# Retention outputs of the later units as 64x64 quads, states without zero blocks, the values in two parts around a drain of TensorE

## The chip, the core and the metric

The kernel runs on one core of a Trainium2 chip. The core has TensorE (PE in the profile; its weight loads are listed apart as PEld), VectorE (DVE), ScalarE (ACT), GpSimd (POOL) and SyncE (SP, which issues most of the DMAs here). The engines run side by side, each taking its own instructions in order, and wait for each other through semaphores. The metric is the device time of one execution in microseconds (us); lower is better.

## The reference

Retention over 8 batches of 8 heads, 576 positions, head size 64, then a two-layer network with ELU over all 4608 tokens (width 512, inner width 2048). Cut to what matters:

```python
scores = scale * np.matmul(q, k.transpose(0, 1, 3, 2))
gamma = 1.0 - 2.0 ** (-5.0 - np.arange(H))
rel = pos[:, None] - pos[None, :]
Dmat = np.where(rel >= 0, gamma[:, None, None] ** rel, 0.0)
attn = np.matmul(scores * Dmat, v)                    # [B, H, S, D]
x = attn.transpose(0, 2, 1, 3).reshape(B * S, H * D)
h = x @ w_in
g = np.where(h > 0, h, np.exp(np.minimum(h, 0)) - 1)
out = g @ w_out
```

The decay splits into a factor for the query's row and one for the key's row. So a run of positions needs only the masked products inside itself and a carried state, the sum of k v^T (64x64 for each head) over all earlier positions, which the queries multiply.

## The kernel before

**Units.** The attention is cut into units: one batch `b`, 256 positions (`T` is 0 or 1, the first or second 256), four heads (`w` is 0 or 1). Eight batches give units 0 to 31 in order of `b`, `T`, `w`; the last 64 positions of each batch go into two tail items, `t0` and `t1`. Units from 12 on (`FAR`, `PAIR`) are "far" ones and go in pairs, `w` 0 and 1 together. A far unit's 256 positions are four chunks of 64, `x = 2 * e + c`: `e` is the 128-row half, `c` the partition half in it.

**What is done for a far unit.** SP loads q, k and v. POOL multiplies q and k by their decay factors into `qkn` in bf16 (`scaled`, L481) and casts v into `vn` (L531). A DMA transposes `qkn` into `qkT` (L585): eight blocks of 128 columns, four of q and four of k, in the order of `qkn`'s free axis, `(i e h d)`. A block is thus two heads (`i` in the code, 64 rows each) of one half `e`.

**Stretches.** PE works on the network most of the time and leaves it for a "stretch" (`stretch`): the outputs of the previous pair (`prevs`) and the beginnings of the next one (`its`), in this order:

- `do_inter`: the carried states times the queries. For each chunk and each pair of heads one 128x128 matmul of 64 columns: the state tile `blocks` holds the two heads' 64x64 states on its diagonal and zeros beside them. Chunk 0 of a unit with T = 0 has no earlier positions, so a pair has 12 such matmuls for T = 0 and 16 for T = 1.
- `do_scores`: 32 matmuls of 64x64 by 64 columns for the next pair, into `sc`.
- `do_values`: 32 such matmuls for the previous pair; masked scores (`pt`) by v, added to what `do_inter` left in the same PSUM tiles, `(xkey, 0)` and `(xkey, 1)`. The tile's number is the chunk's `c`, and the keys of a chunk lie in the partition half `c`, so each half of the array's rows writes one bank alone.
- `do_state`: 32 such matmuls, k by v of the next pair, into two more PSUM tiles.

There are ten stretches with a far pair in `prevs`; in the tenth `its` is the tail item `t0`, which has no states.

**After a stretch.** DVE masks the scores into `pt` (`mask_step`, L890). DVE or ACT adds up the states along the chunks (`after_far`, L834 and L836: `mid` and `end`, f32, 64 rows for each head). Then two copies of 64 partitions by 256 elements write them into the diagonal of `blocks` (`emit_z`, L849), both on the same engine, POOL, DVE or ACT. The zeros of the twelve `blocks` buffers are written once, by memsets around 24 to 40 us (L1172). ACT or DVE copies the outputs into `xt` (`put_two`, L928), which is the network's moving operand: four blocks of 128 features, each with its tokens side by side.

**The network.** `ffn1` (L273 in the profile, through the helper `mm`): 4 matmuls per step into one PSUM bank, 512 tokens wide for the later batches; then exp on ACT (`e`, L1090), max(h, 0) on ACT or DVE (L1098, L1100), and the product on DVE (`g`, L1105). `ffn2`: 16 matmuls of 512 columns for each 128 tokens, a copy to `ot` (L1139) and a store. Six PSUM banks (`"f": 6`) serve both layers, the stretch's x and state tiles, and the early transposes; the scores have the other two.

**Order.** The order on each engine is made while the kernel is built: every piece of work is an `Op` with an assumed cost for each engine that may do it, a rank, the ops that it needs, and the buffers that it takes. `Plan.run` walks through time and gives a free engine the ready op with the lowest rank; on an op with a choice of engines it takes the one that would finish first (the second number of a cost in brackets counts against that engine). `cost_of` and the cost in `stretch` are the assumed times of PE; the chip sees the order alone.

Of the kernel before, what the change touches and what calls it, by code (L numbers as in the profile page):

```python
# [17 lines left out]
P = 128  # L18
# [18 lines left out]
class Plan:  # L37
# [186 lines left out]
PE_TURN = 7  # L224
WG = ("ck11", "ck11", "ck11", "ck12")
WOG = ("ck13", "ck13", "ck13", "ck13")
FREE = ("f", "e", "g", "ot", "z")
LONE = ()

SLOTS = {  # L230
    "f": 6, "sc": 1,
    "rqk": 7, "rv": 6, "qkn": 5, "vn": 6, "qkT": 5, "pt": 3,
    "rqt": 2, "rvt": 2, "qkt": 2, "vt": 4, "qkTt": 8,
    "xt": 3, "g": 28, "e": 4, "ot": 5, "mid": 6, "end": 4, "s_mid": 6, "s_end": 10, "z": 12,
}


# [1 line left out]
def kernel(  # L239
# [234 lines left out]
    def scaled(it, i, e, cost):  # L474
        n = it.n
        key, raw = ("qkn", n), ("rq" + "qk"[i], n)
        g = ((far_q, far_k) if it.far else (gq, gk))[i]
        g = g[:, 2 * it.T + e, 4 * it.w : 4 * it.w + 4].unsqueeze(2).to_broadcast([P, 4, D])

        def emit(op):  # L480
            pin(alu[op.eng].tensor_tensor(tiles[key][:, i, e], tiles[raw][:, :, e], g, ALU.mult))  # L481
# [12 lines left out]
    def scaled_far(it, i, cost):  # L494
        n = it.n
        key, raw = ("qkn", n), ("rq" + "qk"[i], n)
        g = (far_q, far_k)[i][:, 2 * it.T : 2 * it.T + 2, 4 * it.w : 4 * it.w + 4].unsqueeze(3).to_broadcast([P, 2, 4, D])

        def emit(op):
            pin(alu[op.eng].tensor_tensor(tiles[key][:, i], tiles[raw].rearrange("p h e d -> p e h d"), g, ALU.mult))  # L500
# [54 lines left out]

    def flat(n):
        return tiles["qkn", n].rearrange("p i e h d -> p (i e h d)")

    def prepare(it, turn):
        n = it.n  # L560
# [86 lines left out]
    def do_scores(it):  # L647
        n = it.n
        sc = tiles[it.sc]
        if it.tail:  # L650
            for m in range(2):
                for hp in range(HP):
                    for i in range(2):
                        r = slice(i * D, (i + 1) * D)
                        for j in range(2):
                            tt = tiles["qkTt", n, m, j]
                            o = (m * HP + hp) * ST
                            mm(sc[j * ST : (j + 1) * ST, i, o : o + ST], tt[r, hp, ST:], tt[r, hp, :ST],
                               start=True, stop=True)
            return  # L660
        tt = tiles["qkT", n]
        if it.far:
            for x in range(4):
                for i in range(2):
                    r = slice(i * D, (i + 1) * D)
                    for c in range(2):
                        cs = slice(c * C, (c + 1) * C)
                        mm(sc[cs, i, it.sc0 + x * C : it.sc0 + (x + 1) * C], tt[r, 4 + x, cs], tt[r, x, cs], start=True, stop=True)
# [18 lines left out]
    def do_inter(it, xkey, o=0):  # L687
# [9 lines left out]
            return  # L697
        if it.far:
            tt = tiles["qkT", n]
            for x in range(4):  # L700
# [17 lines left out]
    def do_values(it, xkey, x0=0):  # L718
        n = it.n
        if it.tail:  # L720
            pt = tiles["pt", n].rearrange("p i h n -> p i (h n)")
# [10 lines left out]
        if it.far:  # L732
            pt = far_pt(it)
            for hl in range(2):
                for e in range(2):
                    for c in range(2):
                        cs = slice(c * C, (c + 1) * C)
                        o = x0 + hl * P + e * C
                        for i in range(2):
# [11 lines left out]
    def do_state(it, views):  # L751
# [3 lines left out]
        for hl in range(2):  # L755
            for e in range(2):
                for c in range(2):
# [1 line left out]
                    key, bank, ap = views[c]  # L759
                    o = (e * P if it.far else 0) + hl * D  # L760
                    for i in range(2):
                        acc(key, bank, i, ap()[i * D : (i + 1) * D, o : o + D], kn[cs, 1, e, 2 * hl + i],
                            vn[cs, 2 * hl + i, e])

    total = {}

# [53 lines left out]
    def after_far(its, st, view, bank_keys):  # L820
# [5 lines left out]
        for x in range(4):  # L826
# [15 lines left out]
            prev = run, key  # L842
            if m == 2:
                out = key_of(name, b, t, 0, *((x + 1,) if x < 3 else ()))

                def emit_z(op, key=key, out=out):
                    for j in range(2):
# [3 lines left out]
                blk = add(f"b{x}_{n}", {"POOL": 0.8, "DVE": (0.52, 1.0), "ACT": (0.76, 0.6)}, [run, zeros], emit_z, its[0].rank + 3,  # L851
                          take=[T("z", out, [P, 2, 2, P], BF16)], use=[key])
                for it in its:
                    if x < 3:
                        it.bms.append(blk)
                    else:
                        it.be = blk
# [48 lines left out]
    def inter_deps(it):  # L906
        if it.tail:
            return [*it.cvs, *(at[4 * it.t + j, 1, w].be for j in range(4) for w in range(2))]
        return [it.cv, *(it.bms if it.far else [it.bm])] + ([at[it.b, 0, it.w].be] if it.T else [])

    def inter_uses(it):
        if it.tail:
# [5 lines left out]

    xdone, xbegun = {}, set()

    def put_two(its, xkey, dep):

        for c in range(2):
            it = its[0]

            def emit(op, c=c, it=it):
                dst = tiles[it.xt][:, :, it.T * TB : (it.T + 1) * TB].rearrange("p h (e c r) -> p c h e r", e=2, c=2)[:, c]
                pin(copy[op.eng](dst, tiles[xkey, c].rearrange("p (h e r) -> p h e r", e=2, r=C)))  # L928

            first = it.xt not in xbegun  # L930
            xbegun.add(it.xt)
# [5 lines left out]
    def put_x(it, xkey, dep):  # L937

        for c in range(2):
            def emit(op, c=c):  # L940
# [3 lines left out]
                    pin(copy[op.eng](dst, xs.rearrange("p (m h n) -> p m h n", m=2, h=HP)))  # L944
                else:
                    src = xs[:, : 2 * P].rearrange("p (h e r) -> p h e r", h=2, e=2)
                    o = it.T * TB + c * P
                    dst = xt[:, 2 * it.w : 2 * it.w + 2, o : o + P].rearrange("p h (r e) -> p h e r", e=2)
                    if it.far:
                        dst = xt[:, 2 * it.w : 2 * it.w + 2, it.T * TB : (it.T + 1) * TB].rearrange(  # L950
                            "p h (e c r) -> p c h e r", e=2, c=2)[:, c]
                    pin(copy[op.eng](dst, src))  # L952

            first = it.xt not in xbegun
# [29 lines left out]
    def stretch(prevs, its):  # L984
# [86 lines left out]
    def ffn1(blk, p, rank):  # L1071
# [243 lines left out]
```

## Time and profile before

| | |
|---|---|
| time, median of three runs | 301.13 us (300.9 to 301.63) |
| the profiled execution | 301.73 us; span 300.0 us; granted clock 1.0 |
| matmuls of the network, 512 columns | start 0.216 us apart |
| a stretch, first `blocks` matmul to the end of the states' issue | about 1.3 us (T = 0) and 1.4 us (T = 1) |
| `emit_z` copies, 64x256 | POOL 64 at 0.399 us, ACT 16 at 0.404 us |
| `qkn` of far units, 128x256 | POOL 80 at 0.614 us |
| first layer's exp, ACT / max, ACT or DVE / product, DVE | 0.597 / 0.594 or 0.695 / 0.684 us |
| copies to `xt` of a pair, 128x512 | ACT 20 at 0.589 us |
| memsets of `blocks` | DVE 12 at 0.272 us |
| sums of states, 128x256 | DVE 0.415 to 0.425 us |

The page gives for each engine the time in which it was busy. A matmul's duration in it is the time from its start to a modelled end; matmuls of one stream overlap, so what one costs is read from the distance of starts. A line of the timeline is a run of equal instructions: start, length, engine, line, operation, output <- inputs, array size, shape and number; brackets at the end say how long the engine was idle before and who ended that. In the list of waits each line is: engine and line that waited <- who ended it: us in all, times, longest. A few per cent of matmul records are missing from a trace (here 536 of 576 full-width matmuls of the second layer have one), so counts can fall short and a gap of one matmul's length may be none.

### The profile page before, as it was taken

How to read it: one execution, taken by the hardware profiler on the slowest of the kernel's cores; microseconds unless marked ns; L12 is line 12 of the kernel's file. 1: busy time of each engine (PE TensorE's matmuls, PEld its weight loads, DVE VectorE, ACT ScalarE, POOL GpSimd, SP SyncE). 2: the span in 40 equal slices, each digit the busy share in tenths (PEclk: the TensorE clock that was granted, in tenths of full speed). 3: DMA queues.
4: the chain of work that ended last, by engine and by line, in shares of the span. 5: the costliest groups of instructions: out<-in, count | busy, mean ns of one | idle time of the engine just before them, and what ended most of it. 6: DMA issues, size and time to landing. Idle time of an engine off the chain costs nothing.

```text
span 300.0 us, 8468 instructions
## 1 busy us (share of the span) xinstructions
PE 291.4 (97%) x3371; PEld 169.9 (57%) x3405; DVE 174.3 (58%) x312; ACT 194.6 (65%) x379; POOL 145.0 (48%) x276
## 2 busy tenths in 40 slices
PE   8999999899999999999999999999999999999996
PEld 4778746658767764545545544554545444444444
DVE  5979945948756637697755663675442564334300
ACT  2449724827768758787676777768764676777611
POOL 5980389975757838599393974536330000000000
PEclk9999999999999999999999999999999999999999
DMA  7999999999999999999999989876762010011132
GB/s 203 264 206 211 219 294 298 260 196 206 181 169 250 220 177 240 214 214 195 224 209 210 210 188 214 149 170 78 185 147 75 14 38 35 35 35 37 35 106 70
DMA packets 135607, 50.10 MB, mean 167 GB/s; under 512 B 108176, under 2 KB 131088, under 8 KB 135568
## 3 DMA queue, kind: packets, MB, share of 16 engines
q1 hardware_dynamic: 131344, 45.37, 72.7%
q0 software_dynamic: 4224, 4.19, 8.4%
q8 instruction: 26, 0.43, 0.6%
q14 instruction: 13, 0.11, 0.1%
HBM read 36.70 MB, written 9.44 MB: 154 GB/s over the span
## 4 chain that ended last, share of the span: by engine, by line
PE 89%; POOL 3%; DMA 2%; DVE 2%; issue 1%; ACT 0%; ACTq 0%; DVEq 0%
PE f L273 86%; PE sc L273 3%; DMA qkT<-qkn 2%; POOL qkn L481 1%; DVE pt L896 1%; PE f L544 1%; POOL s_end L794 1%; POOL s_mid L794 1%; POOL w_in_sb L459 0%; DVE qkn L481 0%; POOL vn L531 0%; DVE xt L952 0%; DVE qkT L550 0%; DVE s_mid L808 0%; PE f L1276 0%
## 5 line engine op out<-in xcount | busy, mean ns | idle before, releaser
L1105 DVE SCALAR_TENSOR_TENSOR g<-e,f 128x512 bf16<-128x512 f32 x144 | 96.4, 684 | 79.6 <-ACT f L1098 79.0
L273 PE MATMUL f<-w_out_sb,g 128*128 128x512 bf16 (+2 forms) x584 | 138.7, 367 | 2.4 <-issue 1.6
L273 PE MATMUL f<-xt,w_in_sb 128*128 128x256 bf16 (+1 forms) x758 | 139.6, 325 | 0.6 <-DVE xt L952 0.2
L1090 ACT ACTIVATE e<-f 128x512 f32<-128x512 f32 x144 | 85.0, 597 | 47.8 <-PE f L273 39.5
L273 PEld LDWEIGHTS <-w_in_sb 128*128 128x128 bf16 x768 | 74.3, 98 | 53.2 <-DVE xt L952 0.5
L273 PEld LDWEIGHTS <-g 128*128 128x128 bf16 x608 | 56.8, 98 | 58.5
L1098 ACT ACTIVATE f<-f 128x512 f32<-128x512 f32 x122 | 72.2, 594 | 0.0
L1139 ACT COPY ot<-f 128x512 f32<-128x512 f32 (+2 forms) x38 | 21.4, 567 | 19.1 <-PE f L273 16.3
L849 POOL CAST blocks<-mid 64x256 bf16<-64x256 f32 x48 | 19.1, 398 | 18.4 <-DVE mid L836 9.1
L481 POOL TENSOR_TENSOR qkn<-rqk,far_q 128x256 bf16<-128x256 f32 x40 | 24.0, 614 | 7.4 <-DMA rqk<-in_q_dram 6.7
L481 POOL TENSOR_TENSOR qkn<-rqk,far_k 128x256 bf16<-128x256 f32 x40 | 24.1, 614 | 5.5 <-DMA rqk<-in_k_dram 5.0
L531 POOL CAST vn<-rv 128x512 bf16<-128x512 f32 x28 | 17.1, 612 | 15.8 <-DMA rv<-in_v_dram 15.6
L481 POOL TENSOR_TENSOR qkn<-rqk,gq 128x256 bf16<-128x256 f32 x21 | 13.0, 626 | 12.5 <-DMA rqk<-in_q_dram 11.6
L1100 DVE TENSOR_SCALAR f<-f 128x512 f32<-128x512 f32 x22 | 15.3, 695 | 4.3 <-ACT e L1090 4.0
L896 DVE TENSOR_TENSOR pt<-sc,mask 128x1024 bf16<-128x1024 f32 x12 | 14.6, 1216 | 5.3 <-PE sc L273 5.2
L928 ACT CAST xt<-f 128x512 bf16<-128x512 f32 x20 | 10.7, 589 | 9.7 <-PE f L273 9.7
L601 POOL TENSOR_TENSOR qkt<-rqt,gq 128x256 bf16<-128x256 f32 x16 | 9.4, 614 | 12.7 <-DMA rqt<-in_k_dram 12.5
L481 POOL TENSOR_TENSOR qkn<-rqk,gk 128x256 bf16<-128x256 f32 x21 | 12.8, 628 | 2.4 <-DMA rqk<-in_k_dram 2.4
L890 DVE TENSOR_TENSOR pt<-sc,mask_t 128x1024 bf16<-128x1024 f32 x10 | 12.2, 1220 | 2.2 <-PE sc L273 2.2
L952 ACT CAST xt<-f 128x256 bf16<-128x256 f32 x17 | 6.9, 450 | 9.2 <-PE f L273 9.2
L273 PE MATMUL sc<-qkT 64*64 64x64 bf16 (+1 forms) x512 | 9.7, 208 | 0.9 <-DMA qkT<-qkn 0.8
L836 DVE TENSOR_TENSOR mid<-f,mid 128x256 f32<-128x256 f32 x20 | 8.5, 425 | 3.3 <-ACT mid L834 1.0
(88 smaller groups left out, 174.3 us busy)
## 6 DMA issues: line engine op xcount, KB each, us to landing
out_dram<-ot SPq DMA_DIRECT2D x30, 256.0 KB, 3.1
rqk<-in_q_dram SPq DMA_DIRECT2D x40, 128.0 KB, 3.3
rqk<-in_k_dram SPq DMA_DIRECT2D x40, 128.0 KB, 3.3
rv<-in_v_dram SPq DMA_DIRECT2D x40, 128.0 KB, 3.5
rqk<-in_q_dram SPq DMA_DIRECT2D x12, 256.0 KB, 5.5
rqk<-in_k_dram SPq DMA_DIRECT2D x12, 256.0 KB, 5.3
rv<-in_v_dram SPq DMA_DIRECT2D x12, 256.0 KB, 10.2
w_in_sb<-in_moe_w_in_dram POOLq DMA_DIRECT2D x4, 512.0 KB, 9.2
```

The source lines that it names most:

```text
L273: pin(nc.tensor.matmul(*a, **kw))
L481: pin(alu[op.eng].tensor_tensor(tiles[key][:, i, e], tiles[raw][:, :, e], g, ALU.mult))
L531: pin(copy[op.eng](tiles["vn", n], tiles["rv", n]))
L849: pin(copy[op.eng](tiles[out][r, :, :, r], tiles[key][r]))
L890: pin(nc.vector.tensor_tensor(tiles[it.pt].rearrange("p i h n -> p (i h n)")[:, : 2 * w * C].rearrange("p (i x n) -> p i x n", i=2, n=C), ...
L896: pin(nc.vector.tensor_tensor(tiles["pt", n].rearrange("p i h n -> p (i h) n"), tiles[it.sc].rearrange("p i (h n) -> p (i h) n", h=2), mas ...
L928: pin(copy[op.eng](dst, tiles[xkey, c].rearrange("p (h e r) -> p h e r", e=2, r=C)))
L1090: pin(nc.scalar.activation(tiles[ekey], tiles[hkey], AF.Exp))
L1098: pin(nc.scalar.activation(ph, ph, AF.Relu))
L1100: pin(nc.vector.tensor_scalar_max(ph, ph, 0.0))
L1105: pin(nc.vector.scalar_tensor_tensor(tiles[gkey], tiles[ekey], -1.0, tiles[hkey], ALU.add, ALU.min))
L1139: pin(copy[op.eng](tiles[okey][:, :cols], tiles[pkey][:, :cols]))
```

## The change

Far units (12 to 31) alone change, except for the `xt` layout, which changes for all.

1. `qkn` of a far unit gets the order `(i h e d)`, so a block of `qkT` is one head, with `e` = 0 in rows 0 to 63 and `e` = 1 in rows 64 to 127. Scores and states read it accordingly.
2. The carried states are kept as plain 64x64 blocks in a new tile `y`, in the partition half `e` of the chunk that will use them. Both heads of a pair lie beside each other; there are no zeros. Each sum is written by two ops of one copy each, 64 partitions by 256 elements: the one that stays in its partitions may go to POOL, DVE or ACT, the one that crosses partitions to DVE or ACT. Only the last state of a batch (read by the tails) stays a `blocks` tile, so six buffers and six memsets are left of twelve.
3. `do_inter` of a far unit takes four 64x64 matmuls, one for each quadrant of the array (`e` in rows, head `i` in columns), where one of 128x128 stood for two heads: 24 for each T = 0 pair, 32 for each T = 1 pair. The PSUM tile's number is now `e`.
4. With that, half of the values (keys of partition half `c` into tile `e` with `c` different from `e`) would have the other rows of the array write the same bank. `do_values` is called twice: `c = e` straight after the states' products, and the rest after `nc.tensor.drain()` at the end of the stretch. The order in a stretch is now: inter, 16 values, scores, states, drain, 16 values.
5. `xt` holds its tokens by blocks of 128, `(t k n)`: a copy writes 512 contiguous elements, and the first layer's moving operand is four (or two) pieces of 128.
6. The assumed PE cost of a far unit's inter part falls to 0.1, and the order of all engines is planned anew with it.

```diff
-FREE = ("f", "e", "g", "ot", "z")
+FREE = ("f", "e", "g", "ot", "z", "y")
...
-    "xt": 3, "g": 28, "e": 4, "ot": 5, "mid": 6, "end": 4, "s_mid": 6, "s_end": 10, "z": 12,
+    "xt": 3, "g": 28, "e": 4, "ot": 5, "mid": 6, "end": 4, "s_mid": 6, "s_end": 10, "z": 6, "y": 7,
...
+    def by_head(n):
+        return flat(n).rearrange("p (i h e d) -> p i h e d", i=2, h=4, e=2)
...
-            pin(alu[op.eng].tensor_tensor(tiles[key][:, i, e], tiles[raw][:, :, e], g, ALU.mult))
+            dst = by_head(n)[:, i, :, e] if it.far else tiles[key][:, i, e]
+            pin(alu[op.eng].tensor_tensor(dst, tiles[raw][:, :, e], g, ALU.mult))
...
-            for x in range(4):
-                c, e = x % 2, x // 2
-                if it.T + x == 0:
-                    continue
-                s = kept("s_mid", it.b, it.T, it.w, x) if x else kept("s_end", it.b, 0, it.w)
-                for hl in range(2):
-                    acc((xkey, c), 0, 2, tiles[xkey, c][:, o + hl * P + e * C : o + hl * P + (e + 1) * C], s[:, hl],
-                        tt[:, e * 2 + hl, c * C : (c + 1) * C])
+            for hl in range(2):
+                for c in range(2):
+                    for i in range(2):
+                        for e in range(2):
+                            x, r = 2 * e + c, slice(e * D, (e + 1) * D)
+                            if it.T + x == 0:
+                                continue
+                            s = kept("s_mid", it.b, it.T, it.w, x) if x else kept("s_end", it.b, 0, it.w)
+                            at0 = o + hl * P + c * C
+                            acc((xkey, e), 0, i, tiles[xkey, e][i * D : (i + 1) * D, at0 : at0 + C], s[r, 2 * hl + i],
+                                tt[r, 2 * hl + i, c * C : (c + 1) * C])
...
-                for e in range(2):
+                for i in range(2):
                     for c in range(2):
-                        cs = slice(c * C, (c + 1) * C)
-                        o = x0 + hl * P + e * C
-                        for i in range(2):
-                            acc((xkey, c), 0, i, tiles[xkey, c][i * D : (i + 1) * D, o : o + C], vn[cs, 2 * hl + i, e],
-                                pt[cs, i, 2 * e + hl])
+                        cs, e = slice(c * C, (c + 1) * C), c ^ cross
+                        o = x0 + hl * P + c * C
+                        acc((xkey, e), 0, i, tiles[xkey, e][i * D : (i + 1) * D, o : o + C], vn[cs, 2 * hl + i, e],
+                            pt[cs, e, 2 * hl + i])
...
+                if x < 3 or t == 0:
+                    half = slice((x + 1) // 2 % 2 * D, ((x + 1) // 2 % 2 + 1) * D)
+                    blk = []
+                    for j in ((x + 1) // 2 % 2, 1 - (x + 1) // 2 % 2):
+                        def emit_y(op, key=key, out=out, j=j, half=half):
+                            dst = tiles[out].rearrange("p w (l j) d -> p w l j d", j=2)[half, :, :, j]
+                            pin(copy[op.eng](dst, tiles[key][j * D : (j + 1) * D]))
+
+                        cost = {"DVE": (0.3, 0.6), "ACT": (0.4, 0.4)}
+                        blk.append(add(f"b{x}{len(blk)}_{n}", cost if blk else {"POOL": 0.41, **cost}, [run], emit_y,
+                                       its[0].rank + 3, take=[] if blk else [T("y", out, [P, 2, 4, D], BF16)],
+                                       use=[key, *([out] if blk else [])], after=blk[0] if blk else None))
...
+    def by_block(key):
+        return tiles[key].rearrange("p k n -> p (k n)").rearrange("p (t k n) -> p t k n", k=KJ, n=P)
...
-                dst = tiles[it.xt][:, :, it.T * TB : (it.T + 1) * TB].rearrange("p h (e c r) -> p c h e r", e=2, c=2)[:, c]
-                pin(copy[op.eng](dst, tiles[xkey, c].rearrange("p (h e r) -> p h e r", e=2, r=C)))
+                pin(copy[op.eng](by_block(it.xt)[:, 2 * it.T + c], tiles[xkey, c].rearrange("p (h n) -> p h n", n=P)))
...
-            return ("i" in parts) * (0.27 + 0.06 * it.T) + 0.1 * sum(x in parts for x in "svt")
+            return 0.1 * sum(x in parts for x in "isvt")
...
         def emit(op):
+            far = bool(prevs) and prevs[0].far
             for i, it in enumerate(prevs):
                 do_inter(it, xkey, *([i * 2 * P] if len(prevs) > 1 else []))
+            if far:
+                for i, it in enumerate(prevs):
+                    do_values(it, xkey, i * 2 * P, 0)
             for it in its:
                 do_scores(it)
-            for i, it in enumerate(prevs):
-                do_values(it, xkey, *([i * 2 * P] if len(prevs) > 1 else []))
+            if not far:
+                for i, it in enumerate(prevs):
+                    do_values(it, xkey, *([i * 2 * P] if len(prevs) > 1 else []))
             if states:
                 for it in its:
                     do_state(it, view_of(it))
+            if far:
+                pin(nc.tensor.drain())
+                for i, it in enumerate(prevs):
+                    do_values(it, xkey, i * 2 * P, 1)
...
-                    o, x = (ph, xt[:, j]) if wide else (ph[:, f * TB : (f + 1) * TB], xt[:, j, at0 : at0 + TB])
+                    if blk == "T":
+                        o, x = ph, xt[:, j]
+                    else:
+                        x = by_block(xkey)[:, at0 // P : (2 * TB if wide else at0 + TB) // P, j]
+                        o = ph if wide else ph[:, f * TB : (f + 1) * TB]
+                        o = o.rearrange("p (t n) -> p t n", n=P)
```

In the changed order PE's instructions are the same up to the first stretch with a far pair in `prevs`. Behind it the stretches keep their sequence but stand between other MLP matmuls; after the last tail item 52 matmuls of the first layer follow each other, where there were 32.

More of the change, by code (lines that the diff above doesn't have):

```diff
@@ L662, in do_scores @@
         if it.far:
-            for x in range(4):
-                for i in range(2):
-                    r = slice(i * D, (i + 1) * D)
+            for h in range(4):
+                for e in range(2):
+                    r = slice(e * D, (e + 1) * D)
                     for c in range(2):
                         cs = slice(c * C, (c + 1) * C)
-                        mm(sc[cs, i, it.sc0 + x * C : it.sc0 + (x + 1) * C], tt[r, 4 + x, cs], tt[r, x, cs], start=True, stop=True)
+                        mm(sc[cs, e, it.sc0 + h * C : it.sc0 + (h + 1) * C], tt[r, 4 + h, cs], tt[r, h, cs],
+                           start=True, stop=True)
             return
@@ L699, in do_inter @@
             tt = tiles["qkT", n]
-            for x in range(4):
-                c, e = x % 2, x // 2
-                if it.T + x == 0:
-                    continue
-                s = kept("s_mid", it.b, it.T, it.w, x) if x else kept("s_end", it.b, 0, it.w)
-                for hl in range(2):
-                    acc((xkey, c), 0, 2, tiles[xkey, c][:, o + hl * P + e * C : o + hl * P + (e + 1) * C], s[:, hl],
-                        tt[:, e * 2 + hl, c * C : (c + 1) * C])
+            for hl in range(2):
+                for c in range(2):
+                    for i in range(2):
+                        for e in range(2):
+                            x, r = 2 * e + c, slice(e * D, (e + 1) * D)
[5 more added lines that the diff above has]
+                                tt[r, 2 * hl + i, c * C : (c + 1) * C])
             return
@@ L716, in do_inter, with do_values @@
                         queries(n, slice(0, P), hl, c))
-    def do_values(it, xkey, x0=0):
+    def do_values(it, xkey, x0=0, cross=None):
         n = it.n
@@ L761, in do_state @@
                     for i in range(2):
-                        acc(key, bank, i, ap()[i * D : (i + 1) * D, o : o + D], kn[cs, 1, e, 2 * hl + i],
-                            vn[cs, 2 * hl + i, e])
+                        k_of = by_head(n)[cs, 1, 2 * hl + i, e] if it.far else kn[cs, 1, e, 2 * hl + i]
+                        acc(key, bank, i, ap()[i * D : (i + 1) * D, o : o + D], k_of, vn[cs, 2 * hl + i, e])
     total = {}
@@ L844, in after_far @@
                 out = key_of(name, b, t, 0, *((x + 1,) if x < 3 else ()))
+                if x < 3 or t == 0:
[9 more added lines that the diff above has]
+                                       use=[key, *([out] if blk else [])], after=blk[0] if blk else None))
+                    for it in its:
+                        if x < 3:
+                            it.bms += blk
+                        else:
+                            it.be = blk
+                    continue
                 def emit_z(op, key=key, out=out):
@@ L853, in after_far @@
                 for it in its:
[L854 to L857, printed above, removed]
+                    it.be = blk
                 continue
@@ L908, in inter_deps @@
             return [*it.cvs, *(at[4 * it.t + j, 1, w].be for j in range(4) for w in range(2))]
-        return [it.cv, *(it.bms if it.far else [it.bm])] + ([at[it.b, 0, it.w].be] if it.T else [])
+        return [it.cv, *(it.bms if it.far else [it.bm])] + (
+            [] if not it.T else at[it.b, 0, it.w].be if it.far else [at[it.b, 0, it.w].be])
     def inter_uses(it):
@@ L946, in emit @@
                     src = xs[:, : 2 * P].rearrange("p (h e r) -> p h e r", h=2, e=2)
[L947 to L951, printed above, removed]
+                    hs = slice(2 * it.w, 2 * it.w + 2)
+                    dst = by_block(it.xt)[:, 2 * it.T + c, hs].rearrange("p h (r e) -> p h e r", e=2)
                     pin(copy[op.eng](dst, src))
```

7 lines of the change are left out of this document (4 added, 3 removed).

## The prediction

> **What bounds the kernel now.** I read the page first (busy shares, the slices, the chain), then who waited for whom on TensorE (PE), then the timeline of PE in two of the ten stretches that the change touches, then the rows of single operations.
>
> ```profile
> PE 291.4 (97%) x3371; PEld 169.9 (57%) x3405; DVE 174.3 (58%) x312; ACT 194.6 (65%) x379; POOL 145.0 (48%) x276
> PE   8999999899999999999999999999999999999996
> PE 89%; POOL 3%; DMA 2%; DVE 2%; issue 1%; ACT 0%; ACTq 0%; DVEq 0%
> ```
>
> PE is busy 97% of the span and 89% of the chain is PE. A busy PE alone proves little, so the waits:
>
> ```profile
> PE f L273 <- issue: 1.6, 10, 0.2
> PE f L273 <- DVE zero L278: 1.3, 1, 1.3
> PE sc L273 <- DMA qkT<-qkn: 0.8, 1, 0.8
> PE f L544 <- POOL qkn L481: 0.3, 1, 0.3
> PE f L273 <- DVE xt L952: 0.2, 1, 0.2
> ```
>
> The four named releasers lie in the first 60 us. The ten waits on "issue" of 0.16 us are no waits: each stands where PE goes back to 128x128 work, and is the place of one matmul whose record is missing (the next one starts 216 ns, one 512-column matmul, late). So from 60 to 297 us PE issues without a pause, and what the change adds to or takes from PE's own stream moves the end by the same amount. Work on DVE, ACT, POOL and SP counts only if it makes PE wait.
>
> The part at stake is the stretch, in which PE leaves the MLP for the attention of one pair of units. Outputs of a pair with T = 0, then the start of one with T = 1:
>
> ```profile
> 124.25 0.51 PE L273 MATMUL f<-qkT,blocks 128*128 128x64 bf16 x12
> 124.70 0.45 PE L273 MATMUL sc<-qkT 64*64 64x64 bf16 x32
> 124.97 0.44 PE L273 MATMUL f<-pt,vn 64*64 64x64 bf16 x32
> 125.23 0.52 PE L273 MATMUL f<-vn,qkn 64*64 64x64 bf16 x32
> 125.68 0.82 PE L273 MATMUL f<-xt,w_in_sb 128*128 128x512 bf16 x2
> ...
> 110.61 0.63 PE L273 MATMUL f<-qkT,blocks 128*128 128x64 bf16 x16
> 111.17 0.45 PE L273 MATMUL sc<-qkT 64*64 64x64 bf16 x32
> ```
>
> Durations of pipelined matmuls overlap, so I price by starts. Twelve state matmuls take 124.70 - 124.25 = 0.45 us, sixteen 111.17 - 110.61 = 0.56: four more cost 0.11, some 28 ns each (the trace's single starts say 29). 12 x 0.029 = 0.35, so 0.095 of either block is the change from 128x128 to 64x64 work. The 32 scores take 0.27 us, the 32 values 0.26: 8.3 ns per quad matmul. The 32 states take 0.34, and the way back to 128x128 some 0.12.
>
> **The quads.** Removed are the 140 matmuls of `blocks` by `qkT` (5 stretches of 12, 5 of 16); added are 280 of 64x64 (24 and 32). By the scores' row 32 quads cost 0.27. For 24, both lower quadrants still do all eight rounds, so they cost between 24/32 of 0.27 = 0.20 and 0.27; I take 0.24. The 0.095 of the mode change stays; it now comes ahead of the quads instead of behind. Saved: 0.56 - 0.095 - 0.27 = 0.195 for T = 1, 0.45 - 0.095 - 0.24 = 0.115 for T = 0. Sum 5 x 0.195 + 5 x 0.115 = 1.55 us (1.4 to 1.7).
>
> If the quads ran no closer than the matmuls of `blocks`, 29 ns apart, 280 x 29 = 8.1 us would replace 140 x 29 = 4.1, and the part would lose 4.0 us instead; the scores' row, 8.6 ns, contradicts that for quads of four different tiles. A rule of the Trainium skill speaks against the quads too (TensorE: Matmul & The Clock Gate, Part 1): it puts the start-to-start distance of matmuls at no less than about 25 ns, however few columns, by which they would take 7.0 us and lose 2.9. This trace differs from it by a factor of three.
>
> **The drain.** `nc.tensor.drain()` stands in all ten stretches, between the states (the tail's scores in the tenth) and the second half of the values. No drain between matmuls is in this trace. The nearest row is the one at the program's end (rows of its line: times min/median/max in ns, first and last start; then the last matmuls of the timeline):
>
> ```profile
> L1310 PEldq DRAIN  x2: 13/604/1195, 296.1 to 299.6; - x2
> ...
> L1299 PEldq DRAIN  x1: 8/8/8, 0.3 to 0.3; - x1
> ```
>
> ```profile
> 295.77 1.45 PE L273 MATMUL f<-w_out_sb,g 128*128 128x128 bf16 x23
> ```
>
> The long one starts at 296.07, while PE's queue still holds matmuls, and lasts 1.195 us, to 297.27: 0.05 after the last matmul's end (295.77 + 1.45 = 297.22). So a drain holds PE's sequencer until the array is through. A 64-column matmul lasts 0.193 from its start; add that 0.05, and 0.05 until the next instruction starts, as PE restarts after a memset in the chain:
>
> ```profile
> 1.21 0.05 issue
> 1.26 3.17 PE f L273 x7
> ```
>
> The second half of the values then starts 0.29 after the last state instead of 0.01: 0.28 lost, 2.8 us in ten stretches. PE runs in order, so nothing on PE hides it. Queued behind the drain are the 16 values, the whole MLP stream, and the x banks: values used to end ahead of the 32 states, now they end the stretch, so ACT's copies to `xt` start 0.34 later against the MLP stream. In the stretch at 110.61 these copies end at 113.05 and the MLP first reads that `xt` at 113.89; of 0.84 us 0.5 stays, so nothing is added. If ACT is late by more than that, PE waits there, at most two or three times by some tenths.
>
> Bounds. Below: a drain costs what the mode change costs, 0.095, so 0.95 in all; or nothing, as the drain at the start (8 ns, on an empty array). Above: with 0.1 for the sequencer's next step (on PE, 0.10 passes from the end of a semaphore instruction at 299.48 to the drain at 299.58) and 0.04 for 16 values that can no longer be loaded ahead (the states need 0.34 per 32 where the values need 0.26), it is 0.42, so 4.2. I take 0.28, the row of the same instruction, and half of the 0.04, so 0.2, for the slower second half.
>
> For the low bound there is a rule as well: the Trainium skill (TensorEngine Tiling (Array Packing), Tiling Modes) says that changing the tiling mode drains TensorE. By it the 0.095 is the price of a drain, and the sum falls by 2.0 us. What the rule doesn't say is whether an explicit drain, which goes through the sequencer, can be that short; the row at 296.07 says no.
>
> **What lies beside PE, at nothing.** The state copies are 80 before (64 on POOL, 16 on ACT) and 80 after: in the changed order 38 on POOL, 32 on ACT, 10 on DVE. At 0.40 each ACT gains 16 x 0.404 = 6.5 us and loses five relus of 0.594 to DVE; DVE gains those five at 0.695 and ten copies at about 0.415 (its nearest row, 128x256 from PSUM), and loses six memsets of 0.272. ACT goes from 195 to 198 us, DVE from 174 to 180, both far under PE's 291; POOL falls by 10. The copies follow the sums by a few us, and the stretch that reads them comes 7 to 20 us later. The new element order of `qkn` gives POOL a destination in four pieces; strided sources cost it 0.626 against 0.614 without, so 80 x 0.01 on an engine half idle. `xt` by blocks makes the MLP's moving operand four pieces of 128 columns. Scores of early units read two pieces of 64 and repeat every 56 ns per four quads, as do their values, which read 128 in one piece: no price.
>
> PE's order is the same up to the first far stretch; the third stands eight MLP matmuls (1.7 us) earlier. Its last transpose was issued at 118.60 and lands 4.3 us later, 1.8 before the scores at 124.70; with two drains ahead of it that still holds, so nothing. If that cover is gone, it costs what is missing, at most 1 us, once.
>
> **Sum.** -1.55 + 2.8 + 0.2 = +1.45 us. The profiled execution took 301.73 us (span 300.0, 1.7 around it), 0.6 over the median 301.13; it should become 303.2 with a span of 301.5, and the median 302.6.
>
> **The rivals.**
> - The drain is as short as a mode change (0.095). For it: both wait for the array to run empty. Against: the drain at 296.07. -1.55 + 0.95 = -0.6, so 300.5.
> - The other side, faster: the drain holds nobody up, because by the time the sequencer reaches it the array is through, or the matmuls behind it are taken as if it weren't there. For it: 8 ns at the start. Against: PE runs its queue well behind the sequencer (1.2 us at the end). -1.55, so 299.6. It decides once a drain costs under 0.06.
> - ACT and DVE become the bound in long runs of first-layer matmuls. The changed order has 52 in a row (13 steps of 0.864 us) after the last tail, 32 before. Per 13 steps, ACT has 13 exps and 8 relus (21 x 0.597 = 12.5 us), DVE 13 x 0.684 + 5 x 0.695 = 12.4, PE 11.2: they fall 1.3 behind. Six PSUM slots hold 5.2 us, less one in filling and some 2.2 of exp, relu, product (0.60 + 0.59 + 0.68) and hand-offs: 2.1 of slack, so they cover it. If the tail's banks take two slots, 1.7 is gone and PE waits 0.9 there and about as much in the run of 36 in the middle: 304.4.
> - The quads don't overlap, 29 ns apart. Against: the scores' row. 301.13 + 4.0 + 3.0 = 308.1.
>
> **How the numbers follow.** Forecast 0.60 (own range 301.9 to 303.6: drain 0.24 to 0.36), short drain 0.15, free drain 0.12, ACT and DVE 0.12, no overlap 0.01. The range reaches from the short drain to ACT and DVE, 300.5 to 304.4. A measurement tells 0.3%, 0.9 us, from no change. Slower: 0.55 of the forecast plus 0.13 = 0.68; same: 0.05 + 0.15 = 0.20; faster: 0.12.
>
> **What would show it.** The rows of `y` by `qkT` should take 0.27 per 32 by starts; from the last state to the values behind the drain should pass about 0.3 us, ten times; PE's waits should name no engine after 60 us. A gap of 0.1 or less makes it wrong; so do waits on ACT or DVE around 235 us, or quads that start 25 ns or more apart.

## The result, and the profile after

The changed kernel took 304.75 us (median of 4 runs, 303.98 to 305.75) against 301.28 for the kernel before beside it: ratio 1.0112, 95% interval 1.0077 to 1.0147. It is slower, as forecast, but by 3.5 us where 1.45 were forecast, and outside the range. A second measurement, among the experiments below, gave 303.96 against 301.23, ratio 1.0085 (1.0071 to 1.0098): 2.55 us by the ratio (the medians lie 2.73 apart). Both intervals hold 1.0077 to 1.0098, 2.3 to 2.9 us, and that is the loss to be explained.

From the page of the changed kernel: busy time and share by engine, TensorE's (PE's) busy tenths in 40 slices, and the engines' shares of the chain of waits.

```profile
PE 294.8 (97%) x3545; PEld 167.6 (55%) x3545; DVE 179.8 (59%) x322; ACT 196.2 (65%) x389; POOL 135.4 (45%) x250
PE   7999999999899999999999999999999999999996
PE 75%; DMA 14%; POOL 6%; DVE 3%; issue 1%; SPq 1%; ACT 0%; POOLq 0%; ACTq 0%
```

PE still bounds it; ACT, DVE and POOL are about where the prediction put them (198, 180, 135). The fall of PE's share in the chain from 89% to 75% looks like news and is not: the chain in order of time is PE, with the drains between, from 77.45 us to the last matmul, and only before that does it run mostly over transfers and POOL, where executions differ (below). What PE waited for (total us, times, longest us):

```profile
PE f L273 <- issue: 1.7, 8, 0.4
PE f L273 <- DVE zero L278: 1.3, 1, 1.3
PE f L273 <- POOL s_mid L802: 0.9, 1, 0.9
PE sc L273 <- DMA qkT<-qkn: 0.5, 1, 0.5
PE f L273 <- DVE pt L919: 0.2, 1, 0.2
PE f L273 <- DVE vn L533: 0.2, 1, 0.2
PE f L546 <- POOL qkn L482: 0.2, 1, 0.2
```

The named waits end at 77.45 us, with the one on `s_mid`. The prediction's sign, no engine after 60 us, was thus missed by this one wait; in the stretches no engine is named. "issue" now stands for the drains, as the timeline of one stretch shows (start us, us, engine, line, operation; what is in brackets is idle time behind the modelled end):

```profile
111.71 0.45 PE L273 MATMUL f<-qkT,y 64*64 64x64 bf16 x32
111.98 0.30 PE L273 MATMUL f<-pt,vn 64*64 64x64 bf16 x16
112.11 0.47 PE L273 MATMUL sc<-qkT 64*64 64x64 bf16 x32
112.39 0.45 PE L273 MATMUL f<-vn,qkn 64*64 64x64 bf16 x32
113.03 0.32 PE L273 MATMUL f<-pt,vn 64*64 64x64 bf16 x16 [0.19 <-issue]
113.28 0.39 PE L273 MATMUL f<-w_out_sb,g 128*128 128x512 bf16 x1
```

The quads are as forecast: 32 states by query in 111.98 - 111.71 = 0.27 us. Behind the 32 new states the second half of the values starts at 113.03. The states themselves end their starts at 112.66, so 0.37 us pass where 0.01 passes between two quads.

For all runs I use one account of PE's matmul starts: when the first attention stretch after 84 us begins; the time of that and the twelve further stretches up to the end of the attention (each from 0.216 us behind the start of the last MLP matmul ahead to the start of the next MLP matmul, a missing record counted as 0.216); and the rest.

| kernel | first stretch at | 13 stretches | rest | last start |
|---|---|---|---|---|
| before | 85.42 | 17.99 | 193.59 | 297.00 |
| after | 86.18 | 20.16 | 193.67 | 300.01 |

The rest, all MLP matmuls, differs by 0.08 (it is 193.56 to 193.67 in all twelve profiles of this case), so `xt` by blocks, the copies and the new order cost nothing there, as forecast. Of 3.0 us, 0.76 arose before 86 us and 2.17 in the stretches. The first are mostly the wait on `s_mid` (0.9), here in the chain in order of time (start, us, what):

```profile
71.72 4.42 DMA rqk<-in_q_dram
...
76.21 0.61 POOL qkn L482
76.82 0.58 POOL s_mid L802
...
78.08 8.49 PE f L273 x88
```

A load took 4.42 us, POOL took its `qkn` only then and the `s_mid` behind it, and PE waited. The experiments had to settle whether the first belongs to the change, and why the second is not 1.45.

### The profile page after: what moved, and what is told of

Its sections match the earlier page's. It is cut to its first block, busy times and chain, and to the rows that moved or that the text cites. A ratio compares the mean times of both kernels' runs of the same rounds, so it can differ in the third digit from the quotient of the medians.

```text
span 303.0 us, 8828 instructions
## 1 busy us (share of the span) xinstructions
PE 294.8 (97%) x3545; PEld 167.6 (55%) x3545; DVE 179.8 (59%) x322; ACT 196.2 (65%) x389; POOL 135.4 (45%) x250
## 4 chain that ended last, share of the span: by engine, by line
PE 75%; DMA 14%; POOL 6%; DVE 3%; issue 1%; SPq 1%; ACT 0%; POOLq 0%; ACTq 0%
PE f L273 73%; DMA w_out_sb<-in_moe_w_out_dram 7%; POOL qkn L482 2%; DMA qkT<-qkn 2%; PE sc L273 2%; DMA rv<-in_v_dram 2%; DMA rqk<-in_k_dram 2%; DMA rqk<-in_q_dram 1%; DVE pt L919 1%; POOL s_mid L802 1%; POOL s_end L802 1%; POOL w_out_sb L467 1%; POOL vn L533 1%; POOL w_in_sb L459 0%; DVE qkn L482 0%
## 5 line engine op out<-in xcount | busy, mean ns | idle before, releaser
L273 PE MATMUL f<-w_out_sb,g 128*128 128x512 bf16 (+2 forms) x608 | 141.7, 368 | 0.1
L1135 ACT ACTIVATE f<-f 128x512 f32<-128x512 f32 x117 | 69.2, 594 | 0.0
L1137 DVE TENSOR_SCALAR f<-f 128x512 f32<-128x512 f32 x27 | 18.7, 695 | 4.2 <-ACT e L1127 3.9
L859 POOL CAST y<-mid 64x256 bf16<-64x256 f32 x24 | 9.8, 409 | 23.9 <-DVE mid L844 11.3
L954 ACT CAST xt<-f 128x512 bf16<-128x512 f32 x18 | 9.8, 588 | 14.7 <-PE f L273 14.7
L273 PE MATMUL f<-pt,vn 64*64 64x64 bf16 (+1 forms) x512 | 11.5, 204 | 2.2 <-issue 1.7
L859 ACT CAST y<-mid 64x256 bf16<-64x256 f32 x30 | 11.7, 402 | 0.5
```

Source lines behind the costliest of these rows:

```text
L273: pin(nc.tensor.matmul(*a, **kw))
L859: pin(copy[op.eng](dst, tiles[key][j * D : (j + 1) * D]))
L954: pin(copy[op.eng](by_block(it.xt)[:, 2 * it.T + c], tiles[xkey, c].rearrange("p (h n) -> p h n", n=P)))
L1135: pin(nc.scalar.activation(ph, ph, AF.Relu))
L1137: pin(nc.vector.tensor_scalar_max(ph, ph, 0.0))
```

## The experiments

Ten runs: eight new kernels, and both kernels once more. Each was timed beside the kernel before on the same chip.

**A drain alone, in the kernel before.** In all ten stretches:

```diff
             for it in its:
                 do_scores(it)
+            if prevs and prevs[0].far:
+                pin(nc.tensor.drain())
             for i, it in enumerate(prevs):
                 do_values(it, xkey, ...)
```

> The kernel before, with a drain of TensorE in each of the ten stretches of units 12 to 31, between the scores and the values; nothing else is changed. Theory (a drain costs what the changed kernel's trace shows from the last state to the first value behind it, 0.39 us, less the 0.01 that two quads stand apart): ten times 0.38, so 3.8 us, ratio 1.0126, and a gap of 0.37 to 0.39 us from the last score to the first value in each of the ten. Rival (the drain costs the 0.28 of the prediction, and what is missing lies elsewhere): 2.8 us, ratio 1.009. The page's waits stay as before.

Measured: 303.86, ratio 1.0075 (1.0048 to 1.0102). Timeline of its stretch at 110 us, and the row of the drain's line (times min/median/max in ns, first and last start):

```profile
110.63 0.45 PE L273 MATMUL sc<-qkT 64*64 64x64 bf16 x32
111.21 0.44 PE L273 MATMUL f<-pt,vn 64*64 64x64 bf16 x32
111.47 0.49 PE L273 MATMUL f<-vn,qkn 64*64 64x64 bf16 x32
```

```profile
L1016 PEldq DRAIN  x10: 410/414/420, 95.0 to 213.0; - x10
```

From the first score to the first value 0.58 us pass instead of 0.27. The single starts give a gap of 0.326 or 0.327 in nine of ten (0.329 in the other) instead of 0.022, and the states behind take 0.30 instead of 0.34. The 13 stretches take 20.74, against 17.93 in a second profile of the kernel before: 0.28 per drain. So the theory with 0.38 fell; at this place the prediction's 0.28 is right, in part by luck: the gap grew by 0.30, and the faster states give 0.03 back. The starts also show its parts: the drain ends 0.073 us after the last score's modelled end, and the next matmul starts 0.060 after that (0.05 and 0.05 had been put in).

**The drains taken out.** VectorE copies one element of an x bank behind the first half, and the second half, which writes that bank, waits for the copy; this keeps the halves in order.

```diff
+    spare = const.tile([1, 2], FP32, name="spare")
...
                     do_values(it, xkey, i * 2 * P, 0)
+                pin(nc.vector.tensor_copy(spare[:, :1], tiles[xkey, 1][:1, :1]))
...
-                pin(nc.tensor.drain())
```

> The changed kernel without its ten drains. In the place of each drain VectorE copies one element of the x bank behind the first half of the values, and the second half waits for that copy, so the halves stay in order; between them lie the scores and states, about 0.55 us. Theory (the drain is the whole loss): the gap from the last state to the second half falls from 0.39 to 0.01 us where the copy comes in time, so 3.8 us come back, 301.0, ratio to the kernel before 0.999; if VectorE takes the copy late by 0.2 to 0.3 us in every stretch, as an operation of 0.6 us may stand ahead of it, 303 to 304. Rival (the drain is worth 2.8 and the rest is the changed order): 302.0 where the copies come in time, ratio 1.003.

Measured: 300.51, ratio 0.9976 (0.9954 to 0.9998).

```profile
110.11 0.47 PE L273 MATMUL sc<-qkT 64*64 64x64 bf16 x32
110.40 0.47 PE L273 MATMUL f<-vn,qkn 64*64 64x64 bf16 x32
110.69 0.34 PE L273 MATMUL f<-pt,vn 64*64 64x64 bf16 x16
```

```profile
L1041 DVE COPY spare<-f x10: 145/145/147, 95.1 to 214.3; 1x1 f32<-1x1 f32 x10
```

The second half follows the first state by 0.29 us instead of 0.64. The copy takes 0.145 us and is in time in nine stretches; in the tenth, where no states lie between the halves, the second half starts 0.18 behind the last score instead of 0.02. The stretches take 17.40 us, 2.85 less than in the changed kernel measured again (below). The time lies under both numbers that were expected where the copies come in time, 301.0 and 302.0: the gaps are the theory's, the 2.85 us are close to the rival's 2.8, and the rest of the difference in time lies outside the stretches. The same with ScalarE's copy:

> The changed kernel without drains, the second half of the values waiting for a copy of one element of the x bank by ScalarE (with VectorE in this place the time was 300.5, ratio 0.998). Theory (all that the drains cost comes back, whoever does the copy, if it is there within the 0.55 us of scores and states): 300.2 to 300.8 with a gap of 0.01 us in nine stretches. Rival (ScalarE takes it late, behind an exp or a relu of 0.6 us): gaps of 0.1 to 0.5 us in most stretches, 301 to 303.

Measured: 300.49, ratio 0.9976 (0.9964 to 0.9989), stretches 17.42, a gap of 0.01 in nine: theory. Both versions beat both kernels.

**Two drains in a row.** The line is there twice.

> The changed kernel with two drains in a row in place of each. Theory (a drain costs the emptying of the array, which the second finds empty, and a step of the sequencer): the second adds at most 0.1 us, so 0 to 1 us in ten, 304.8 to 305.8. Rival (each drain has a fixed price of its own): 0.38 more each, 3.8 us, 308.5.

Measured: 303.89, ratio 1.0093 (1.0061 to 1.0125). That is under the 304.8 to 305.8 expected, which had been counted from the first measurement of the changed kernel, and too wide to tell the two apart; the trace does.

```profile
L1050 PEldq DRAIN  x10: 13/13/13, 97.0 to 219.3; - x10
```

The second drain lasts 13 ns and lengthens the usual gap from 0.373 to 0.451: 0.08. So the rival's fixed price of 0.38 falls: most of a drain's price is the emptying of the array, and the rest is this step.

**The drain ahead of the scores.**

```diff
                     do_values(it, xkey, i * 2 * P, 0)
+                pin(nc.tensor.drain())
...
-                pin(nc.tensor.drain())
```

> The changed kernel with the drain right behind the first half of the values, ahead of the scores, instead of behind the states; the second half of the values follows the states at once. Theory (a drain waits for what the array still holds; behind the states it ends 0.126 us after their last modelled end, behind the scores only 0.073): a gap of 0.32 to 0.33 us at the drain, 0.01 from the states to the second half, and 0.03 to 0.05 us less per stretch, so 0.3 to 0.5 us under the changed kernel. Rival (the price of a drain doesn't hang on its place): no difference.

Measured: 302.99, ratio 1.0065 (1.005 to 1.0079), 0.97 us under the changed kernel; stretches 19.38 against 20.25. More came back than the theory gave. Gaps of 0.32 stand in three stretches and 0.305 in the last, but 0.355 in three and 0.40 to 0.44 in the other three. So at the drain the theory's 0.32 to 0.33 came in three stretches only. What came back beside it are pauses inside the rows of quads: there are none over 0.045 us in this kernel, and 0.67 of the 0.87 us come from stretches six, eight, nine and ten, where the changed kernel measured again has its pauses and longest gaps. That they matter was not in any theory so far.

**The planner's cost alone.** The kernel before with the changed cost of a stretch, and the changed kernel with the old one:

```diff
-            return ("i" in parts) * (0.27 + 0.06 * it.T) + 0.1 * sum(x in parts for x in "svt")
+            return 0.1 * sum(x in parts for x in "isvt")
```

> The kernel before, with the changed kernel's cost of a stretch in the planner (the order of instructions changes, the work doesn't). Theory (the order is worth nothing, and the early wait of 0.9 us on POOL at 76 us is a late transfer of that one execution): 301.2, ratio 0.997 to 1.003. Rival (the order planned for shorter stretches brings the early wait and the rest of the loss): about 0.8 us slower, ratio 1.0025 or more, and a wait of PE on POOL of 0.5 us or more near 76 us in its trace.

> The changed kernel with the planner's old cost of a stretch, so the order of its instructions is planned as for the kernel before; the work is the changed kernel's. Theory (order is worth nothing): the same as the changed kernel within 0.3%. Rival (the order brings 0.7 us or more of the loss): 0.7 us or more under it.

Measured: 300.89, ratio 0.9992 (0.9966 to 1.0018), no wait of PE on POOL over 0.4 us in its trace; and 304.13, ratio 1.0101 (1.0077 to 1.0125). The order by itself is worth nothing that these can tell.

**Both kernels again.**

> The changed kernel itself, once more, beside the others. Theory (its steady loss is in the ten stretches, where its trace shows 2.2 us more than the kernel before, and the 0.8 us that it lost before 86 us is a late transfer of that execution, as the first stretch begins at 84.5 and at 85.7 us in two kernels with the same instructions up to there): 303.4, ratio 1.0065 to 1.0085. Rival (the early loss belongs to the change): 304.7, ratio 1.0115, and a first stretch at 86 us or later in its trace.

> The kernel before itself, once more, as a measure of scatter. Theory (what stands ahead of 86 us scatters by 0.8 us between executions and the rest doesn't): ratio 0.999 to 1.001; a first stretch between 84.5 and 86.2 us; at most one pause of 0.06 us or more inside the ten stretches, and their sum with the three others 17.8 to 18.0 us. Rival (the stretches scatter as well): a sum off by 0.3 us or more.

Measured: 303.96, ratio 1.0085 (1.0071 to 1.0098), first stretch at 85.50, so between the two times that were expected, with the first stretch ahead of the rival's 86; and 301.19, ratio 0.9998 (0.9981 to 1.0014), first stretch at 86.08. So the unchanged kernel, too, comes as late as the changed one did in the first profile. The longest of its waits there:

```profile
PE f L273 <- ACT vn L531: 1.7, 1, 1.7
```

One `vn` that came 1.7 us late in this profile is not in the list of the first one. Over all profiles the first stretch begins between 84.2 and 86.1 us in the kernel before and its variants (five) and between 84.5 and 88.0 in the changed kernel and its variants (seven). The two versions without drains say that this is scatter: their instructions are those of the changed kernel up to the stretches, and over 25 runs they took 0.7 us less than the kernel before, of which the stretches explain some 0.55. A loss ahead of the stretches that belongs to the change would have made them slower than that, as far as an interval of 0.4 us to either side tells.

**Longer rows of quads in the kernel before.** The account of the starts shows single steps of 0.06 to 0.18 us inside rows of 64x64 matmuls, at no semaphore and not at a drain. To see whether the row's length brings them, the scores of the ten stretches are issued twice:

```diff
-            for it in its:
+            for it in its * (2 if prevs and prevs[0].far else 1):
                 do_scores(it)
```

> The kernel before, with the 32 scores of each of the ten stretches issued twice (the second time they write the same values), so that 128 matmuls of 64x64 follow each other (96 in the last) instead of 96 (64). Theory (a long row of quads outruns what feeds TensorE's queue: seven kernels with 112 to 120 quads in a row show pauses of 0.06 to 0.16 us inside them, 0.3 to 0.7 us in all, three with 96 in a row only one of 0.11): 2.7 us for the scores, and pauses of 0.06 us or more in at least three of the ten stretches, none ahead of the 57th quad, so 3.0 to 3.4 us more than the kernel before, ratio 1.010 to 1.011. Rival (the pauses come from the state copies and the changed order, not from the row's length): 2.7 us and at most one pause, ratio 1.009.

Measured: 304.23, ratio 1.0099 (1.008 to 1.0118); stretches 21.30, 3.37 more than in the kernel before again. Two stretches of the same kind from its timeline, behind their 12 state matmuls:

```profile
146.59 0.71 PE L273 MATMUL sc<-qkT 64*64 64x64 bf16 x64
147.12 0.45 PE L273 MATMUL f<-pt,vn 64*64 64x64 bf16 x32
147.39 0.52 PE L273 MATMUL f<-vn,qkn 64*64 64x64 bf16 x32
...
170.93 0.71 PE L273 MATMUL sc<-qkT 64*64 64x64 bf16 x64
171.46 0.45 PE L273 MATMUL f<-pt,vn 64*64 64x64 bf16 x32
171.73 0.67 PE L273 MATMUL f<-vn,qkn 64*64 64x64 bf16 x32
```

The same 128 quads; only the states last 0.67 instead of 0.52, for a pause of 0.142 between two of them. Such a pause stands in five of the ten stretches (0.095, 0.142, 0.114, 0.182, 0.134), none ahead of the 80th quad of its row. Scores twice cost 0.267 in a clean stretch (1.697 against 1.430), 2.7 in ten; the pauses bring the remaining 0.7. The time alone, 2.4 to 3.6 us by its interval, fits theory and rival. The trace doesn't fit the rival, at most one pause, and the order on every engine is that of the kernel before here, but for the doubled scores. (The expectation counts the earlier rows as 112 to 120 quads; they are 104 to 128, and in the kernel with the drain ahead of the scores 40 to 80, without a pause.)

The single starts tell more. Each row begins in groups of four, one quad for each quadrant of the array: steps of 3, 4, 3 and 22 ns as a rule, so a quadrant starts a quad every 32 ns. Between the 51st and the 63rd quad the groups end, in every row that neither a drain nor a wait cuts before, and even steps of 8 to 9 ns follow, with longer ones of 17 to 34 among them. All 30 pauses of 0.06 us or more that no semaphore explains, in nine profiles, stand behind the last group of their row; behind a drain the groups are back. This looks like a lead of waiting instructions that a row uses up, so that a late instruction is felt only behind it; that reading fits all rows here, but no run tested it.

## Why the prediction was right and wrong

The account for the ten stretches, per stretch, from those without a pause (kernel before again; without drains; changed kernel again): with T = 0 1.430, 1.337, 1.65; with T = 1 1.547, 1.37, 1.69.

- **The quads** were right. They save 1.430 - 1.337 = 0.09 and 1.547 - 1.37 = 0.18, the slower second half included: 5 x 0.09 + 5 x 0.18 = 1.35. The prediction's terms, -1.55 + 0.2, are -1.35. That the net fits so well is in part chance: in the drainless kernel the 32 scores start over 0.28 us instead of 0.25 and the 32 states over 0.28 instead of 0.34, and neither was forecast. That matmuls can't start closer than some 25 ns, as the Trainium skill has it (TensorE: Matmul & The Clock Gate, Part 1), does not hold for the new rows as a whole, which start 8 ns apart on average. For one quadrant it holds, at 32 ns; the prediction compared the rule with all four at once.
- **The drain** was right in its mechanism and a little small. Behind the states it costs 1.65 - 1.337 = 0.31 and 1.69 - 1.37 = 0.32, so 3.15 instead of 2.8. The gap alone, 0.37 as a rule, overstates it: with the drain the rows ahead of and behind it run 0.05 faster by their starts. Behind the scores it costs 0.28. The gaps differ by how late the drain ends after the last modelled end ahead of it, 0.126 behind states against 0.073 behind scores; why states leave the array later was not tried. Where a pause stands among the states just ahead (stretch eight of the changed kernel, in both its profiles), it is only 0.05 to 0.06, as if there were a backlog that a pause works off.
- **The short drain and the free drain**, rivals, are out. The mode change ahead of the quads is 0.094 and the drain 0.28 to 0.32. The Trainium skill's rule that a change of tiling mode drains TensorE (TensorEngine Tiling (Array Packing), Tiling Modes) is therefore no price for an explicit drain.
- **ACT and DVE as the bound**, a rival, is out: no wait of PE on them after 60 us in the list above (the two of 0.2 us on DVE stand at 7 and 13 us). `xt` by blocks, the copies and the moved order cost nothing: rest 193.67 against 193.59. (The transpose at 118.60 landed 3.6 us later in its own row, not 4.3, which is the median of all; so it had 2.5 us of cover, not 1.8, and nothing hung on it.)
- **What failed** is the sum's premise that "from 60 to 297 us PE issues without a pause", carried over to longer rows of quads: each of the 280 was priced at 8.3 ns of issue, and pauses at nothing. The rows of 64x64 matmuls grew from 96 to 104 and 112 ahead of the drain (64 to 80 in the tenth stretch; 120 and 128 without drains), and in such rows stand pauses, none over 0.06 us ahead of the 57th quad. In the changed kernel measured again the 13 stretches take 20.25, 2.32 more than in the kernel before again; quads and drains give -1.35 + 3.15 = 1.8, so some 0.5 is theirs. They stand in stretches eight, nine and ten; in six and nine the gap at the drain is 0.448 and 0.543 instead of 0.373. Two stretches of the same kind from that timeline, the fourth and the eighth, with the states and the values behind the drain:

```profile
136.65 0.45 PE L273 MATMUL f<-vn,qkn 64*64 64x64 bf16 x32
137.29 0.32 PE L273 MATMUL f<-pt,vn 64*64 64x64 bf16 x16 [0.19 <-issue]
...
192.65 0.58 PE L273 MATMUL f<-vn,qkn 64*64 64x64 bf16 x32
193.34 0.32 PE L273 MATMUL f<-pt,vn 64*64 64x64 bf16 x16
```

The trace of before had one, 0.108 us at 135.44, that the prediction passed over. There the states last 0.64 us, where they last 0.52 in the stretch that the prediction shows:

```profile
135.42 0.64 PE L273 MATMUL f<-vn,qkn 64*64 64x64 bf16 x32
```

The doubled scores show that the row is enough to bring them. Against the 1.45 forecast, then, the drain adds 0.35 and the pauses 0.5: 2.3.

With these 2.3 the second measurement, 2.55 (2.1 to 3.0), is accounted for; the first, 3.5 (2.3 to 4.4), only at its lower edge. The 0.76 us lost before 86 us in that profile lie within the scatter of early transfers, as the kernel before shows the same lateness in one of its own profiles. That the rest of the first measurement is such scatter is likely, as the versions without drains show no early loss, but not shown. What makes a pause is open. It moves from stretch to stretch between kernels with the same rows, and where a drain cuts the row in two ahead of the scores or of the old values (32 to 48 quads ahead of it, at most 80 behind) none was seen inside.

## What to carry to other kernels

A drain on the engine that sets the end costs what is still in the array plus its restart, 0.3 us each time here; where only two of the engine's own writes must be kept in order, a one-element copy by another engine that reads the first and is waited for by the second orders them for nothing, if enough work lies between. Price a long run of very short instructions by more than its issue rate (here pauses came from about the 57th on), and look for single late starts in the trace before. And measure a kernel twice before explaining its last microsecond: the part of a start that hangs on transfers scattered by more than half of this effect.

## What the runs showed of the hardware

Behind a drain's end the next weight load starts after 54 ns and the next matmul after 60, wherever the drain stands, unless a second drain follows. A drain that finds the array empty lasts 13 ns and costs 80.

Instructions come in over the DMA engines. The page's part 3 has a row (packets, MB, share of 16 engines) that the counts below tie to TensorE; here for the changed kernel and, second, for the doubled scores:

```profile
q8 instruction: 27, 0.44, 0.6%
```

```profile
q8 instruction: 29, 0.48, 0.7%
```

The kernel before has 26, with (3371 + 3405) recorded matmuls and weight loads, so a packet of some 16 KB brings about 260 instructions; 320 more scores with their weight loads made it 29. A row of 128 quads is 256 instructions in about 1.1 us. The Trainium skill (Runtime: NRT & Kernel Launch, Instruction fetch mechanics) says that instructions are fetched ahead in blocks of 16 KiB, 256 instructions, which agrees, and that the fetch is hidden because the sequencer dispatches more slowly than the buffer is refilled. Whether the pauses are a fetch that was not hidden no run here shows. Against a plain wait for a packet speak the packets' own times: in the changed kernel measured again two packets start at 193.92 and 204.14 us, while the pauses of those stretches begin at 192.73 and 202.84 and last 0.12 and 0.09, so they are over by then. It is the same for all 30 pauses: no packet of q8 is under way in any, and the next one starts 0.4 to 2.6 us after the pause begins.
